# Dense PSUM banks emptied with a priority, one add moved to GpSimd and an early table load in an attention and gated-MLP kernel

## The chip, the cores and the metric

The kernel runs on one core of a Trainium2 chip. The metric is device microseconds of one execution, the median of several. A core has five engines that run their own instruction lists in order: TensorE (PE, matmul), VectorE (DVE), ScalarE (ACT), GpSimd (POOL) and SyncE (SP, which issues the transfers here). They wait for each other by semaphores alone.

## The reference

Banded causal attention with a linear bias, and two gated blocks behind it, all in float32. Batch 4, 8 heads, 576 positions, 64 values a head; the band is 128 wide.

```python
scores = scale * np.matmul(q, k.transpose(0, 1, 3, 2))
scores = np.where(mask, scores + bias[None], -1e9)      # mask: 0 <= i - j < 128
attn = np.exp(scores - np.max(scores, axis=-1, keepdims=True))
x = np.matmul(attn / (np.sum(attn, axis=-1, keepdims=True) + 1e-09), v)   # -> 2304 x 512
x = (1.0 / (1.0 + np.exp(-(x @ w_gate))) * (x @ w_val)) @ w_out   # 512 -> 1536 -> 512
x = ((x @ w1) * (x @ w2)) @ w3 @ w_out2                           # 512 -> 1024 -> 512
```

## The kernel before

The 2304 positions are cut into five blocks (`TILES`: 256, then four of 512), the eight heads into four pairs. Attention is 20 steps, step n being block n // 4 and pair n % 4. A step has three stages that run in different turns of the loop. `stage_s(n)` makes the scores on PE, masks them and adds the bias table on DVE (lines 446 and 449), takes the maximum (455), and on ACT four exponentials for each pair of tiles with their sums (462); then DVE makes the reciprocals (466), and POOL (470) and ACT (472) scale half of the tiles each. `stage_p(n)` transposes the result on PE (480, tiles pt), copies it out on ACT (act_copy, line 69, tiles cp) and zeroes triangles on POOL (484, 488). `stage_pv(n)` multiplies by v on PE (503, tiles pv) and empties that bank into xt as a rounded high part on ACT (69) and a low part on DVE (72). A turn n runs `stage_p(n-2)`, `stage_pv(n-3)`, `stage_s(n)`, and the first seven turns have an order of their own.

The dense work is `layer(grp, blk)`: `gv` makes two products (tiles gv, line 243), empties the first with a sigmoid on ACT (257, tile g), multiplies the second into it on DVE (262), and splits the result into a high part on ACT (69) and a low part on POOL (75, tiles gt); `down1` multiplies by w_out (280, tiles dn) and adds into acc, by an ACT copy for the first group and a DVE add for the others (289). Pieces of `layer` are put between the attention stages by `fill`, as many matmuls as a budget lets in. So PE's order in the attention is written out by hand (`manual_schedule`). On the other engines a scheduler sets the order from a priority, which follows the program's order, and from its own estimate of when an instruction can run.

Transposes, pv, gv and dn all take their PSUM from one ring of four banks, `mm`; the scores have four banks of their own. A matmul group that comes to a bank waits until what lies there has been emptied:

```python
gvpool = ctx.enter_context(
    tc.tile_pool(name="psmm", bufs=4, space=PSUM, side="right", reuse_waits="tile"))
mmpools.append(gvpool)
```

ACT holds one table of functions at a time. The exponential and the sigmoid are in different ones, so every sigmoid in the attention has a load ahead of it (ACT_TABLE_LOAD), and the next exponential another.

The weights arrive as 64-bit floats and are converted by a chain on ACT (115), DVE (116 to 121) and ACT, POOL or DVE again (`convert_next`), with a low priority: `LATER` puts them behind other work. At the start `consts` builds the bias table base on POOL, with one add on DVE (369), and `table(0)` scales it on ACT (404, tiles tab). After the attention all is dense work, and PE's list is the program's order.

Of the kernel before, what the change touches and what calls it, by code (L numbers as in the profile page):

```python
# [9 lines left out]
F32 = mybir.dt.float32  # L10
# [3 lines left out]
AF = mybir.ActivationFunctionType  # L14
ALU = mybir.AluOpType
# [4 lines left out]
P = 128  # L20
# [9 lines left out]

PASSES = ((0, 0), (0, 1), (1, 0))
LATER = 300
FILL = {5: 0.0, 6: 1400.0, 7: 1400.0, 8: 0.0, 9: 0.0, 10: 2700.0, 11: 2700.0}
FULL = 4000.0

# [10 lines left out]
def attn_moe_kernel(  # L46
# [14 lines left out]
    nc = tc.nc  # L61
# [6 lines left out]
    def act_copy(dst, src):  # L68
        nc.scalar.activation(dst, src, AF.Copy)  # L69
# [4 lines left out]
    def pool_lo(dst, src, hi):  # L74
        nc.gpsimd.tensor_tensor(dst, src, hi.bitcast(F32), ALU.subtract)  # L75
# [10 lines left out]
    def cols(blk):  # L86
        return TILES[blk] * P
# [36 lines left out]
    def convert_next():  # L124

        key, _, sink = queue.pop(0)
        with tc.high_priority(offset=-LATER):
            t = staged.pop(key)
# [10 lines left out]
    def convert_start(items):  # L139
        queue.extend(items)  # L140
        for it in queue[:2]:
            if it[0] not in staged:
                fetch(*it[:2])
# [13 lines left out]
    def parts(grp):  # L157
        def src(i, c):
            m = i - NF
            own = (w_gate, w_val, w_out)[c][i] if i < NF else (w1[m], w2[m], w3o[m * P : (m + 1) * P, :])[c]  # L160
            return ahead.get((i, c), own)

        keys = [(i, c) for c in range(3) for i in grp]
        return [(key, src(*key), part_sink) for key in keys]
# [67 lines left out]
    def gv(grp, blk, xs, one):  # L232

        pss = {}
        w = cols(blk)
        ns = w / 2.4 + 13.3

        def product(i, s):
            full = gvpool.tile([P, TB], F32, tag=gvtag, name=f"gv{i}_{blk}_{s}", bufs=gvbufs)
            ps = pss[i, s] = full[:, 0:w]  # L240
            for kk in range(NK):
                for wp, xp in PASSES:
                    nc.tensor.matmul(  # L243
                        ps,
                        wsl[i][:, s, wp, kk * P : (kk + 1) * P],
                        xs[blk][:, xp, kk],
                        start=(kk == 0 and wp == 0 and xp == 0),
                        stop=(kk == NK - 1 and wp == 1),
                    )
                yield 3 * ns  # L250

        g = {}
        for i in grp:
            yield from product(i, 0)
        for i in grp:
            g[i] = m2.tile([P, TB], F32, tag="g", name=f"g{i}_{blk}")[:, 0:w]
            nc.scalar.activation(g[i], pss[i, 0], AF.Sigmoid if one else AF.Copy)  # L257
        ts = []
        for i in grp:
            yield from product(i, 1)  # L260
            pr = g[i]
            nc.vector.tensor_tensor(pr, pr, pss[i, 1], ALU.mult)  # L262
            t = m2.tile([P, 2, TB], F32R, tag="gt", name=f"gt{i}_{blk}", bufs=4)[:, :, 0:w]
            act_copy(t[:, 0], pr)
            pool_lo(t[:, 1], pr, t[:, 0])
            ts.append(t)
        return ts

    def down1(grp, blk, ts):
        first, last = grp[0] == 0, grp[-1] == NF - 1  # L270
        if first:
            acc[blk] = acc_tile(blk, [P, NK, cols(blk)], "acc1")
        if last:
            x2.append(x_tile("x2_", blk))
        for m in range(NK):
            ps = mm_tile([P, TB], f"dn{grp[0]}_{blk}_{m}")[:, 0 : cols(blk)]
            n = 0
            for i, t in zip(grp, ts):
                for wp, xp in PASSES:
                    nc.tensor.matmul(  # L280
                        ps, wsl[i][:, 2, wp, m * P : (m + 1) * P], t[:, xp],
                        start=n == 0, stop=n == 3 * len(grp) - 1,
                    )
                    n += 1
            a = acc[blk][:, m]
            if first:
                act_copy(a, ps)
            else:
                nc.vector.tensor_tensor(a, a, ps, ALU.add)  # L289
            if last:  # L290
                act_copy(x2[blk][:, 0, m], a)
                dve_lo(x2[blk][:, 1, m], a, x2[blk][:, 0, m])
            yield 3 * len(grp) * (cols(blk) / 2.4 + 13.3)
# [36 lines left out]
    def attention(actx, conv):  # L330
        nonlocal spool, gvpool
        cpool = actx.enter_context(tc.tile_pool(name="cpool", bufs=1))
# [15 lines left out]
        def consts():  # L348


            normal0, first, normal, normal2, cross, after, normal3 = (base[:, i] for i in range(7))
            nc.gpsimd.memset(mask, 1)
            nc.gpsimd.affine_select(
                out=mask, in_=mask, compare_op=ALU.is_gt, fill=0.0, base=0, pattern=[[1, P]], channel_multiplier=-1
            )
            for t, k in ((first, 0), (normal, -P)):
                nc.gpsimd.iota(
                    t, pattern=[[1, P]], base=k, channel_multiplier=-1, allow_small_or_imprecise_dtypes=True
                )
            nc.gpsimd.affine_select(  # L360
                out=cross, in_=first, compare_op=ALU.is_ge, fill=0.0, base=0, pattern=[[-1, P]], channel_multiplier=1
            )
            nc.gpsimd.affine_select(
                out=normal, in_=normal, compare_op=ALU.is_gt, fill=0.0, base=0, pattern=[[1, P]], channel_multiplier=-1
            )
            nc.gpsimd.affine_select(
                out=first, in_=first, compare_op=ALU.is_ge, fill=FAR, base=0, pattern=[[-1, P]], channel_multiplier=1
            )
            nc.vector.tensor_tensor(normal, normal, cross, ALU.add)

        def consts2():
            normal0, first, normal, normal2, cross, after, normal3 = (base[:, i] for i in range(7))
# [35 lines left out]
        def load(n):  # L408
            pair, blk, nt, t0, back = where(n)
            t = loads[n]  # L410
            t["k"] = ap2.tile([P, 5 * P], F32, tag="ldk", name=f"ldk{n}")
            t["q"] = ap2.tile([P, 4 * P], F32, tag="ldq", name=f"ldq{n}")

            if not back:
                nc.sync.dma_start(t["k"][:, 0:P], kt[pair, :, t0 * P : (t0 + 1) * P])
            nc.sync.dma_start(t["k"][:, (1 - back) * P : (1 + nt) * P], kt[pair, :, (t0 - back) * P : (t0 + nt) * P])
            nc.sync.dma_start(t["q"][:, 0 : nt * P], qt[pair, :, t0 * P : (t0 + nt) * P])
# [117 lines left out]

        load(0)
        load(1)
        convert_start(parts(groups[0]) + parts(groups[1]) + second_items)
        consts()
        make_identity(nc, ident)  # L540
        table(0)
        with tc.manual_schedule(engines={mybir.EngineType.PE}):
            for n in range(NSTEP + 3):
# [18 lines left out]
                for grp, blk in READY.get(n, ()):  # L562
                    fillers.append(layer(groups[grp], blk))
                fill(FILL.get(n, FULL))
                for _ in range(CONVERT.get(n, 0)):
# [4 lines left out]
    with ExitStack() as conv, ExitStack() as actx:  # L570
        attention(actx, conv)
# [110 lines left out]
```

## Time and profile before

| what | us |
|---|---|
| three runs, median (lowest to highest) | 945.8 (945.59 to 946.12) |
| the profiled execution, its own time | 945.88 |
| its span, first to last instruction | 944.2 |
| PE, ACT, DVE, POOL busy | 897.6, 366.9, 573.5, 290.6 |
| last transposes of the attention start at | 192.5 |
| last pv starts at | 199.7 |
| mean granted TensorE clock | 0.979 |

The span and the execution's own time differ by 1.7 us. The profile shows when each instruction ran and, for idle time ahead of it, whose semaphore ended it. A busy PE is not PE at its peak, since matmuls are pipelined. The granted clock is in shares of full speed, 1.00 for 2.4 GHz; its other level is half of that, and a mean between them is a stretch with both.

### The profile page before, as it was taken

What the parts mean: (1) busy time and instruction counts of PE and PEld (TensorE: products, weight loads), DVE (VectorE), ACT (ScalarE), POOL (GpSimd) and SP (SyncE); (2) the same over time, 40 slices, a digit from 0 to 9 for tenths busy, and PEclk for the clock granted to TensorE, in tenths of its full rate; (3) what the DMA queues carried; (4) which work ended last, traced back from release to release, by engine and by line L of the source; (5) the groups of instructions that cost most, each with busy time, mean ns of one, the idle gap of its engine ahead of it and who ended that gap; (6) DMA issues with size and microseconds to landing.
All of it is one profiled execution on the core that took longest, in us unless ns stands there. A gap on an engine that the chain in (4) does not pass through costs nothing.

```text
span 944.2 us, 12323 instructions
## 1 busy us (share of the span) xinstructions
PE 897.6 (95%) x4528; PEld 736.6 (78%) x4528; DVE 573.5 (61%) x957; ACT 366.9 (39%) x912; POOL 290.6 (31%) x343
## 2 busy tenths in 40 slices
PE   6788786899999999999999999999999999999998
PEld 3456665678878888888888888888888888888887
DVE  5769686525998797698593458943854514422223
ACT  6799897643333332322331244434322312211110
POOL 4567454242422412322322021104422412411111
PEclk9789898999999999999999999999999999999999
DMA  6445353114243243143130122325310300000112
GB/s 185 150 140 161 99 159 119 40 34 145 79 143 113 67 135 101 45 144 113 45 100 23 46 67 101 112 78 156 97 39 1 112 1 1 23 0 1 45 45 112
DMA packets 32604, 79.71 MB, mean 84 GB/s; under 512 B 3616, under 2 KB 5664, under 8 KB 32544
## 3 DMA queue, kind: packets, MB, share of 16 engines
q1 hardware_dynamic: 32544, 78.92, 26.0%
q8 instruction: 36, 0.59, 0.3%
q14 instruction: 24, 0.20, 0.1%
HBM read 65.27 MB, written 13.63 MB: 84 GB/s over the span
## 4 chain that ended last, share of the span: by engine, by line
PE 73%; DVE 11%; ACT 8%; DMA 4%; issue 4%; POOL 1%; SPq 0%; ACTq 0%; POOLq 0%; DVEq 0%
PE gv L243 43%; PE dn L280 11%; PE o L304 10%; PE w3o L209 4%; ACT sm L462 3%; PE pv L503 2%; DVE acc L289 1%; PE s L438 1%; PE pt L480 1%; ACT sm L472 1%; DVE sm L449 1%; DVE s L446 1%; DVE mn L455 1%; ACT cp L69 1%; POOL wsl L75 1%
## 5 line engine op out<-in xcount | busy, mean ns | idle before, releaser
L243 PE MATMUL gv<-xt,wsl 128*128 128x512 f32 (+1 forms) x1440 | 307.6, 372 | 3.2 <-DVE g L262 1.9
L243 PEld LDWEIGHTS gv<-xt,wsl 128*128 128x128 f32 x1440 | 252.5, 191 | 52.7 <-DVE g L262 3.0
L75 POOL TENSOR_TENSOR gt<-g,gt 128x512 fp32r<-128x512 f32 (+1 forms) x100 | 120.5, 1209 | 430.1 <-ACT gt L69 422.8
L243 PE MATMUL gv<-x,wsl 128*128 128x512 f32 (+1 forms) x960 | 200.2, 368 | 0.0
L243 PEld LDWEIGHTS gv<-x,wsl 128*128 128x128 f32 x960 | 167.6, 189 | 30.2
L262 DVE TENSOR_TENSOR g<-g,gv 128x512 f32<-128x512 f32 (+1 forms) x100 | 62.6, 630 | 168.1 <-PE gv L243 151.1
L280 PE MATMUL dn<-gt,wsl 128*128 128x512 f32 (+1 forms) x720 | 156.3, 371 | 5.0 <-ACT cp L69 3.1
L280 PEld LDWEIGHTS dn<-gt,wsl 128*128 128x128 f32 x720 | 126.4, 189 | 30.1 <-ACT cp L69 3.7
L257 ACT ACTIVATE g<-gv 128x512 f32<-128x512 f32 (+1 forms) x100 | 54.7, 550 | 156.1 <-PE gv L243 150.9
L69 ACT ACTIVATE gt<-g 128x512 fp32r<-128x512 f32 (+1 forms) x100 | 58.5, 587 | 145.4 <-DVE g L262 145.2
L304 PE MATMUL o<-wsl,gt 128*128 128x512 f32 x432 | 101.1, 389 | 0.0
L304 PEld LDWEIGHTS o<-wsl,gt 128*128 128x128 f32 x432 | 80.9, 188 | 16.7
L289 DVE TENSOR_TENSOR acc<-acc,dn 128x512 f32<-128x512 f32 (+1 forms) x120 | 74.1, 628 | 21.8 <-PE dn L280 21.5
L313 DVE TENSOR_TENSOR acc<-acc,o 128x512 f32<-128x512 f32 x54 | 37.1, 688 | 35.2 <-PE o L304 35.2
L462 ACT ACTIVATE sm<-sm,mn 128x128 f32<-128x128 f32 x144 | 55.9, 391 | 1.6 <-DVE mn L455 1.0
L503 PE MATMUL pv<-cp,ldv 128*64 128x256 f32 (+1 forms) x352 | 43.4, 382 | 12.6 <-issue 6.9
L503 PEld LDWEIGHTS pv<-cp,ldv 128*64 128x64 f32 x352 | 27.1, 154 | 29.2 <-issue 12.9
L438 PE MATMUL s<-ldk,ldq 64*128 64x256 f32 x288 | 42.1, 434 | 6.3 <-DMA ldq<-in_q_dram 6.3
L470 POOL TENSOR_SCALAR sm<-sm,su 128x128 f32<-128x128 f32 x72 | 32.6, 464 | 41.4 <-DVE su L466 41.4
L209 PE MATMUL w3o<-wo,w3s 128*128 128x512 f32 x192 | 44.4, 390 | 0.2 <-DVE wo L72 0.2
L209 PEld LDWEIGHTS w3o<-wo,w3s 128*128 128x128 f32 x192 | 36.0, 188 | 8.1 <-DVE wo L72 0.7
L438 PEld LDWEIGHTS s<-ldk,ldq 64*128 64x128 f32 x288 | 29.5, 209 | 14.1 <-issue 10.6
(742 smaller groups left out, 868.7 us busy)
## 6 DMA issues: line engine op xcount, KB each, us to landing
ldk<-in_k_dram SPq DMA_DIRECT2D x16, 320.0 KB, 3.0
ldv<-in_v_dram SPq DMA_DIRECT2D x16, 320.0 KB, 2.9
out_dram<-acc SPq DMA_DIRECT2D x18, 256.0 KB, 2.0
ldq<-in_q_dram SPq DMA_DIRECT2D x16, 256.0 KB, 3.3
w3o<-w3os SPq DMA_DIRECT2D x8, 256.0 KB, 2.5
ldk<-in_k_dram SPq DMA_DIRECT2D x4, 128.0 KB, 2.9
ldq<-in_q_dram SPq DMA_DIRECT2D x4, 128.0 KB, 3.0
raw_(0, 0)_99<-in_w_gate_dram SPq DMA_DIRECT2D x1, 512.0 KB, 4.6
```

The costliest lines, as they stand in the source:

```text
L69: nc.scalar.activation(dst, src, AF.Copy)
L75: nc.gpsimd.tensor_tensor(dst, src, hi.bitcast(F32), ALU.subtract)
L209: nc.tensor.matmul(acc2, w3s[u][:, wp, i * P : (i + 1) * P], wo2[kk][:, xp], start=(kk == 0 and wp == 0 and xp == 0), stop=(kk == NC2 - 1 ...
L243: nc.tensor.matmul(ps, wsl[i][:, s, wp, kk * P : (kk + 1) * P], xs[blk][:, xp, kk], start=(kk == 0 and wp == 0 and xp == 0), stop=(kk == N ...
L257: nc.scalar.activation(g[i], pss[i, 0], AF.Sigmoid if one else AF.Copy)
L262: nc.vector.tensor_tensor(pr, pr, pss[i, 1], ALU.mult)
L280: nc.tensor.matmul(ps, wsl[i][:, 2, wp, m * P : (m + 1) * P], t[:, xp], start=n == 0, stop=n == 3 * len(grp) - 1,)
L289: nc.vector.tensor_tensor(a, a, ps, ALU.add)
L304: nc.tensor.matmul(ps, t[:, xp, tt * P : (tt + 1) * P], wsl[i][:, 2, wp], start=n == 0, stop=n == 3 * len(grp) - 1,)
L438: nc.tensor.matmul(ps[:, h, :, u], ld["q"][r, t * P : (t + 1) * P], ld["k"][r, t * P : (t + 2) * P], start=True, stop=True, skip_group_che ...
L462: s["act"] = nc.scalar.activation(y, y, AF.Exp, bias=mn[:, j : j + 1], scale=1.0 / up, accum_out=su[:, j : j + 1])
L503: nc.tensor.matmul(ps[c, a:b], loads[n]["v"][:, j + 1, c], s["cp", h][:, m0 : m0 + b - a], start=j == -back, stop=j == nt - 1, skip_group_ ...
```

## The change

Three edits. The instructions that empty banks of the dense work (sigmoid, multiply, the split, and the add into acc) get a priority 150 places ahead of their place in the program. The add that ends the table base goes from DVE to POOL. An exponential of one column is put on ACT ahead of everything, with a DVE memset for its input.

```diff
+SOONER = 150
@@ gv
-            nc.scalar.activation(g[i], pss[i, 0], AF.Sigmoid if one else AF.Copy)
+            with tc.high_priority(offset=SOONER):
+                nc.scalar.activation(g[i], pss[i, 0], AF.Sigmoid if one else AF.Copy)
@@ gv
-            nc.vector.tensor_tensor(pr, pr, pss[i, 1], ALU.mult)
             t = m2.tile([P, 2, TB], F32R, tag="gt", name=f"gt{i}_{blk}", bufs=4)[:, :, 0:w]
-            act_copy(t[:, 0], pr)
-            pool_lo(t[:, 1], pr, t[:, 0])
+            with tc.high_priority(offset=SOONER):
+                nc.vector.tensor_tensor(pr, pr, pss[i, 1], ALU.mult)
+                act_copy(t[:, 0], pr)
+                pool_lo(t[:, 1], pr, t[:, 0])
@@ down1
-            if first:
-                act_copy(a, ps)
-            else:
-                nc.vector.tensor_tensor(a, a, ps, ALU.add)
+            with tc.high_priority(offset=SOONER):
+                if first:
+                    act_copy(a, ps)
+                else:
+                    nc.vector.tensor_tensor(a, a, ps, ALU.add)
@@ consts
-            nc.vector.tensor_tensor(normal, normal, cross, ALU.add)
+            nc.gpsimd.tensor_tensor(normal, normal, cross, ALU.add)
@@ ahead of convert_start
+        warm = cpool.tile([P, 1], F32, name="warm")
+        nc.vector.memset(warm, 0.0)
+        nc.scalar.activation(warm, warm, AF.Exp)
```

PE's list stays the same but for two matmuls of gv0_4_0. The lists of ACT, DVE, POOL and SP change up to the end of the attention, and hardly after it. Names in the rows below carry the step or the group and block, and a buffer number at the end. ACT keeps its number of table loads, 14. The lines of the changed file stand a few higher: 70 is 69 of before, 259 is 257, 466 is 462, 476 is 472.

First, ACT at steps 4 and 5: sm4 are the exponentials of step 4, cp2 and cp3 the copies of the transposes of steps 2 and 3. Before:

```order
L462 ACTIVATE sm4_314,su4_0_328<-sm4_314,mn4_0_327 128x128 x4
L69 ACTIVATE xt0_278<-pv1_355 128x256
L465 ACTIVATE su4_0_328<-su4_0_328 128x4
L462 ACTIVATE sm4_314,su4_1_343<-sm4_314,mn4_1_342 128x128 x2
L472 ACTIVATE sm4_314<-sm4_314,su4_0_328 128x128 x2
L462 ACTIVATE sm4_314,su4_1_343<-sm4_314,mn4_1_342 128x128 x2
L69 ACTIVATE cp2_0_365<-pt2_0_362 128x2x128
L465 ACTIVATE su4_1_343<-su4_1_343 128x4
L69 ACTIVATE cp2_1_372<-pt2_1_369 128x2x128
L69 ACTIVATE cp3_0_385<-pt3_0_382 128x2x128
```

And of the change:

```order
L70 ACTIVATE wsl0_195<-a_(0, 0)_186 128x512
L70 ACTIVATE xt0_281<-pv1_358 128x256
L70 ACTIVATE cp2_0_368<-pt2_0_365 128x2x128
L70 ACTIVATE cp2_1_375<-pt2_1_372 128x2x128
L70 ACTIVATE cp3_0_388<-pt3_0_385 128x2x128
L466 ACTIVATE sm4_317,su4_0_331<-sm4_317,mn4_0_330 128x128 x4
L70 ACTIVATE cp3_1_395<-pt3_1_392 128x2x128
L469 ACTIVATE su4_0_331<-su4_0_331 128x4
```

The copies cp2 and cp3 went from behind the eight exponentials of step 4 to ahead of them.

Second, ACT where the first sigmoid stands, g0_0, which empties gv0_0_0. Before:

```order
L472 ACTIVATE sm6_495<-sm6_495,su6_1_525 128x128 x2
L257 ACT_TABLE_LOAD
L257 ACTIVATE g0_0_632<-gv0_0_0_538 128x256
L459 ACTIVATE mn7_0_602<-mn7_0_602 128x4
L69 ACTIVATE wsl0_192<-a_(0, 2)_453 128x512
L462 ACT_TABLE_LOAD
L462 ACTIVATE sm7_589,su7_0_603<-sm7_589,mn7_0_602 128x128 x4
```

And of the change:

```order
L463 ACTIVATE mn6_0_511<-mn6_0_511 128x4
L466 ACTIVATE sm6_498,su6_0_512<-sm6_498,mn6_0_511 128x128
L259 ACT_TABLE_LOAD
L259 ACTIVATE g0_0_635<-gv0_0_0_541 128x256
L476 ACTIVATE sm5_406<-sm5_406,su5_1_436 128x128 x2
L466 ACT_TABLE_LOAD
L466 ACTIVATE sm6_498,su6_0_512<-sm6_498,mn6_0_511 128x128 x3
L463 ACTIVATE mn6_1_527<-mn6_1_527 128x4
```

It went from between two softmaxes into that of step 6, and with it both table loads; half of sm5's scaling (line 476) now stands behind the sigmoid.

Third, ACT at step 13: acc1_1 are the four copies that empty dn0_1_0 to dn0_1_3. Before:

```order
L69 ACTIVATE acc1_1_1282<-dn0_1_0_1283 128x512
L459 ACTIVATE mn13_0_1248<-mn13_0_1248 128x4
L69 ACTIVATE acc1_1_1282<-dn0_1_1_1288 128x512
L462 ACT_TABLE_LOAD
L462 ACTIVATE sm13_1235,su13_0_1249<-sm13_1235,mn13_0_1248 128x128 x4
L459 ACTIVATE mn13_1_1264<-mn13_1_1264 128x4
L69 ACTIVATE acc1_1_1282<-dn0_1_2_1293 128x512
L465 ACTIVATE su13_0_1249<-su13_0_1249 128x4
```

And of the change:

```order
L70 ACTIVATE xt2_985<-pv10_1225 128x512
L70 ACTIVATE wsl1_737<-a_(1, 2)_937 128x512
L70 ACTIVATE acc1_1_1285<-dn0_1_0_1286 128x512
L70 ACTIVATE acc1_1_1285<-dn0_1_1_1291 128x512
L463 ACTIVATE mn13_0_1251<-mn13_0_1251 128x4
L70 ACTIVATE acc1_1_1285<-dn0_1_2_1296 128x512
L466 ACTIVATE sm13_1238,su13_0_1252<-sm13_1238,mn13_0_1251 128x128
L70 ACTIVATE acc1_1_1285<-dn0_1_3_1301 128x512
L466 ACTIVATE sm13_1238,su13_0_1252<-sm13_1238,mn13_0_1251 128x128 x3
```

Two of the copies came out from behind the exponentials of step 13, and the table load went away from ahead of them (it stands in step 12 now).

## Rows read from the trace of the kernel before

**Rows 1.** The page: the span.

```profile
span 944.2 us, 12323 instructions
```

**Rows 2.** Windows: us, then busy time of PE, PEld, DVE, ACT, POOL, PEclk, DMA.

```profile
24.00:48.00 24.00, 17.64 (x114) 11.84 (x112) 17.79 (x35) 17.39 (x76) 13.72 (x26) 0.79 0.43 142
48.00:96.00 48.00, 40.35 (x284) 29.03 (x280) 39.41 (x73) 44.71 (x164) 33.63 (x59) 0.89 0.49 160
206.00:300.00 94.00, 92.08 (x439) 76.89 (x438) 77.64 (x125) 30.09 (x53) 29.57 (x23) 1.00 0.37 121
300.00:944.20 644.20, 640.23 (x3048) 539.19 (x3047) 362.54 (x581) 177.44 (x305) 155.03 (x124) 1.00 0.21 67
```

**Rows 3.** PE's waits up to 206 us: us in total, times, longest.

```profile
PE pv L503 <- issue: 6.9, 3, 3.1
PE pv L503 <- POOL cp L488: 5.4, 4, 2.6
```

**Rows 4.** DVE at the start, timeline: start, us, instruction, idle before.

```profile
7.00 0.29 DVE L369 TENSOR_TENSOR base<-base 128x128 f32<-128x128 f32 x1
8.46 0.70 DVE L446 COPY_PREDICATED s<-mask,s 128x512 f32<-128x512 int32 x1 [1.17 <-PE s L438]
9.42 0.69 DVE L449 SCALAR_TENSOR_TENSOR sm<-s,tab 128x512 f32<-128x512 f32 x1 [0.26 <-ACT tab L404]
```

**Rows 5.** The page: groups by line, busy and mean ns of one.

```profile
L75 POOL TENSOR_TENSOR gt<-g,gt 128x512 fp32r<-128x512 f32 (+1 forms) x100 | 120.5, 1209 | 430.1 <-ACT gt L69 422.8
L462 ACT ACTIVATE sm<-sm,mn 128x128 f32<-128x128 f32 x144 | 55.9, 391 | 1.6 <-DVE mn L455 1.0
```

**Rows 6.** PE in order of time.

```profile
23.73 0.86 PE L503 MATMUL pv<-cp,ldv 128*64 128x256 f32 x6 [0.33 <-POOL cp L488]
...
31.86 1.54 PE L503 MATMUL pv<-cp,ldv 128*64 128x256 f32 x6 [1.09 <-POOL cp L488]
33.33 3.79 PE L438 MATMUL s<-ldk,ldq 64*128 64x256 f32 x16
...
38.35 1.09 PE L480 MATMUL pt<-ident,sm 128*128 128x128 f32 x8
39.37 2.00 PE L438 MATMUL s<-ldk,ldq 64*128 64x256 f32 x16
...
45.65 1.95 PE L503 MATMUL pv<-cp,ldv 128*64 128x128 f32 x20
...
97.36 2.93 PE L243 MATMUL gv<-xt,wsl 128*128 128x256 f32 x12 [1.01 <-ACT acc L69]
...
115.06 1.95 PE L503 MATMUL pv<-cp,ldv 128*64 128x128 f32 x20 [2.93 <-issue]
...
125.04 1.95 PE L503 MATMUL pv<-cp,ldv 128*64 128x128 f32 x20 [0.92 <-issue]
...
159.73 1.94 PE L480 MATMUL pt<-ident,sm 128*128 128x128 f32 x8 [6.93 <-ACT acc L69]
...
175.11 3.38 PE L503 MATMUL pv<-cp,ldv 128*64 128x128 f32 x20 [3.07 <-issue]
...
199.68 1.95 PE L503 MATMUL pv<-cp,ldv 128*64 128x128 f32 x20
```

**Rows 7.** ACT in order of time.

```profile
27.89 0.37 ACT L69 ACTIVATE cp<-pt 128x256 f32<-128x256 f32 x1
...
50.61 1.28 ACT L257 ACT_TABLE_LOAD   x1
51.90 0.38 ACT L257 ACTIVATE g<-gv 128x256 f32<-128x256 f32 x1
...
114.39 0.57 ACT L69 ACTIVATE acc<-dn 128x512 f32<-128x512 f32 x1
...
159.01 2.04 ACT L69 ACTIVATE acc<-dn 128x512 f32<-128x512 f32 x4
...
174.41 0.60 ACT L257 ACTIVATE g<-gv 128x512 f32<-128x512 f32 x1
```

## The prediction

> **What bounds the kernel now.** The execution took 945.88 us, 1.7 more than its span [rows 1], and the median of the three runs is 945.8; I reckon from 945.9. First I read busy time by stretch. From 300 us on PE is busy 640.2 of 644.2 us, from 206 to 300 us 92.1 of 94 [rows 2]: dense work, nothing to win. So the change can only be worth what it pulls forward the last pv of the attention, which starts at 199.7 [rows 6]. What stands behind it (weights by DMA, ACT and POOL, then DVE's conversions) is released by ACT and POOL work that itself waits for these last banks, so I let all of it move along with PE.
>
> Next I read PE's waits up to 206 us [rows 3]. They are short and spread: for a bank that ACT has not emptied, for triangles on POOL, for the scaling of the softmax. The reader is to see that there is no single one. Last comes the order of time on PE and ACT [rows 6, 7]: each long wait is an ACT list that does exponentials first, and a copy that PE needs behind them. ACT itself is busy 44.7 of the 48 us from 48 to 96 [rows 2]; there its work in sum, not its order, is close to the limit.
>
> **The method.** I walk the new lists in order, each instruction with its duration in the trace, and write down when PE reaches certain groups. Shifts are against the trace of before; minus is earlier. Copies are 0.37 for 256 columns, 0.57 for 512; four exponentials 4 x 0.39 = 1.56 [rows 5, 7].
>
> **The start (+1.6).** The add on DVE took 0.29 [rows 4]. On POOL no such row exists; a POOL add of 512 columns takes about 1.2 [rows 5]. Between 0.29 and 1.2 I take a quarter of 1.2, 0.3, by columns; either end is free, since DVE's second mask copy comes at 8.46 anyway [rows 4]. The added memset and exponential of one column have no rows either; nothing and the 0.39 of a full exponential [rows 5] bound them, and either is free while the first transfers run. The scale-and-add of step 0 waits today for the table, to 9.42. But DVE's new list has the second mask copy ahead of it, as the old one, and that ends at 8.46 + 0.70 = 9.16 [rows 4]. So the early table load, 1.28, is worth only 0.26. It is more than lost: the first reciprocal now stands behind step 2's mask copy and scale-and-add on DVE, and the second copy of step 0's transposes behind step 2's exponentials on ACT. My walk has pv1's last six matmuls at 25.3, not 23.73 [rows 6].
>
> **Steps 2 to 4 (-4.8).** Today cp2 stands behind eight exponentials of step 4 and comes at 27.89 [rows 7]; pv2's last six run at 31.86, and PE is then at its lower clock (0.79 in the mean from 24 to 48 us [rows 2]): the 16 score matmuls at 33.33 take 3.79, those at 39.37 2.00 [rows 6]. In the new list cp2 comes right behind pv1's copy. That copy ends at 26.6, cp2's first at 27.0, and POOL's four triangles of 0.4 follow without a scaling between: pv2's last at 28.6. Scores then end at 31.4, and step 4's exponentials (27.8 on), its reciprocals and scaling at 33.5, when pt4 can end what starts today at 38.35.
>
> **Steps 5 to 8 (half of it is given back).** g0_0 and two loads, 1.28 + 0.38 + 1.28 = 2.9, move into step 6's softmax, ahead of the ACT half of step 5's scaling and of most of step 6's exponentials. So pt5's last tiles wait for ACT, until 43.3 in my walk, and pv4 starts at 43.6 where it starts at 45.65 now [rows 6]: -2.0. Its cover before was that both loads stood where only step 7 waited; step 7 gets them back, and its transposes come 2.5 earlier.
>
> **Steps 9 to 12 (-5.3).** ACT runs through here nearly without idle time in both lists. g0_1's loads move up by one softmax in the same manner. Then the exponentials of step 11 and the copies cp10, for whose banks dn0_0 waits, come some 5 us earlier, and the four acc1_0 copies stand together. gv1_0_0, now at 97.36 [rows 6], starts at 92.1.
>
> **Steps 13 and 14 (-8.3, then -6.6).** pv11 waits 2.93 for a bank that the third acc1_1 copy frees, at 114.39, behind a load and four exponentials [rows 6, 7]. In the new list this copy is ahead of both: 1.28 + 1.56 = 2.8 less, pv11 at 106.8 for 115.06. But pv12 waits for g0_2, which keeps its place behind step 14's exponentials, so ACT, not PE, sets it: 118.4 for 125.04. 1.7 are given back as idle time.
>
> **Steps 15 to 18 (-7.4).** The adds into acc1_0 come without a scale-and-add and a maximum between them (-0.5). The largest wait, 6.93 at 159.73, stays: the acc1_2 copies (159.01) stand behind step 17's softmax in both lists [rows 6, 7]. It lasts from step 17's scores on, so it moves with them; DVE no longer holds step 17's first scale-and-add for a reciprocal, some 0.6.
>
> **Steps 19 to 22 (-10.3).** pv16 waits 3.07 for g0_3, which ends behind four exponentials at 174.41 + 0.60 [rows 6, 7]. The new list has it ahead of them and of one scaling: 1.56 + 0.34 = 1.9, to -9.4. Step 19 needs no load ahead of its exponentials any more; its last transposes come another 0.9 earlier, and the last pv with them: 189.4 for 199.7 [rows 6].
>
> The walk takes 0.1 for a hand-over between engines. At 9.16 to 9.42 one takes 0.26 [rows 4]; some twelve hand-overs stand on this way, 12 x 0.15 = 1.8 less gain. **Sum: 945.9 - 10.3 + 1.8 = 937.4, and I say 937.5.** A measurement of this kernel can tell about 0.2%, 1.9 us, from no change.
>
> **The price of a switch.** Each pair of loads is priced at 2 x 1.28: the sigmoid starts 0.01 after its load ends [rows 7], so nothing else is paid. The Trainium skill (ScalarE: Activation LUTs, What ACT_TABLE_LOAD costs) gives 1.28 us for a load and 1.38 for a drain with it; by that, the three pairs that now stand ahead of a wait of PE (g0_0, g0_1, g1_0) would cost 3 x 2 x 1.38 = 8.3 more, and the sum would be about 945.8. The trace does not agree: no 1.38 lies beside this load.
>
> **Rivals.**
> *ACT takes it back* (0.16). From 48 to 96 us ACT has only 3.3 us of idle time [rows 2]. If the lead of steps 2 to 4 is used up there, what stays is the bank waits behind it: 2.8 at pv11 less 1.7 at pv12, 1.9 at pv16, 0.6: 942.3. For it speaks the half given back already at step 5; against it that DVE and PE, not ACT, hold several of those exponentials today.
> *Nothing happens* (0.09). The sum of ACT's work and loads is the same and the longest wait stays. If each wait of PE only moves to the next bank or the next scaling, 945.9 within 1.5. Against it: the copies at 27.89 and 114.39 stand behind work that the next PE group doesn't need.
> *A switch costs more in the middle of a softmax* (0.02). If ACT stood still for as long again as the load, 1.28, whenever it changes table between exponentials, the three pairs would cost 3 x 2 x 1.28 = 7.7 more: 945.2. The 0.01 above speaks against it [rows 7]. It is the drain of the skill's section named above.
> *Slower: loads in the middle of a softmax* (0.09). Each early sigmoid puts 2.9 us into a softmax whose scaling the next transposes wait for. It is free as long as PE's groups up to those transposes take longer than that. It decides at step 5: if pt4 is not early, by pv2 still late behind POOL, the 1.6 of the start stay, pt5 ends 2.8 later than now, and the wait that grows at pv12 is 1.7 beyond today's, with 2.8 back at pv11: 945.9 + 1.6 + 2.8 + 1.7 - 2.8 = 949.2.
> *My forecast, faster by 4.5 to 13* (0.64). More than the walk is possible if PE keeps its clock where it loses it today: the 20 matmuls at 175.11 take 3.38 and those at 115.06 1.95 [rows 6], 1.4 each time, at two or three places.
>
> **How the numbers follow.** The likeliest case gives 937.5, its own range 932 to 941.5. Below 932 only several more stretches at full clock lead: 0.06. Up to 944.5 lie nearly all of the first rival and a part of the others. So the range is 932 to 944.5, which leaves out some 2 in 10. Faster by over 0.2% (under 944): my forecast, nearly all of the first rival and a little of the second, 0.80. Within 0.2%: most of the second and the third, 0.11. Slower: 0.09.
>
> **What would show it.** In the trace of the change: pt4 near 34 and the scores of step 5 at 2.0; pv4 near 43.6 (the loss at step 5); gv1_0_0 near 92; no wait ahead of pv11, but one of over 2 ahead of pv12; still some 7 us ahead of pt16; about 1 ahead of pv16; the last pv near 190. From there to the end the distance should be the same as now, 944.2 - 199.7 = 744.5; if it grew, DVE's conversions would have become late, and the forecast would be wrong in that step. It would be wrong in the first step if the scores of step 5 ran at the lower clock or pv2 came after 30.

## The result, and the profile after

The changed kernel takes 936.36 us (median of 4 runs, 935.53 to 939.69); the kernel before, timed beside it, 945.96 (4 runs, 945.59 to 946.89). The ratio is 0.9904, 95% interval 0.9879 to 0.9929: faster, as forecast, and 1.1 us from the 937.5 that was said. The profiled execution took 935.53, its span 933.8.

The stretches, as in [rows 2]: length, then busy time of PE, PEld, DVE, ACT, POOL, granted clock, DMA share, GB/s.

```profile
24.00:48.00 24.00, 19.19 (x130) 13.26 (x128) 20.34 (x39) 20.78 (x78) 15.82 (x30) 0.88 0.54 172
48.00:96.00 48.00, 39.68 (x290) 28.97 (x289) 37.14 (x72) 44.24 (x167) 33.33 (x61) 0.95 0.46 143
196.00:290.00 94.00, 94.00 (x454) 79.42 (x453) 78.70 (x127) 32.18 (x56) 30.02 (x23) 1.00 0.38 123
290.00:933.80 643.80, 639.70 (x3042) 538.23 (x3040) 361.06 (x579) 176.86 (x305) 154.93 (x124) 1.00 0.21 67
```

The dense part is as it was (639.70 for 640.23 us of PE). ACT still has under 4 us to spare from 48 to 96. The third line is new: PE is busy in all 94 us behind the attention, where it lacked 1.9 before [rows 2].

PE's waits up to 196 us (us in total, times, longest):

```profile
PE pt L484 <- POOL sm L474: 10.7, 8, 2.5
...
PE pt L484 <- ACT acc L70: 5.9, 1, 5.9
PE pv L507 <- POOL cp L492: 3.2, 2, 2.5
PE dn L283 <- ACT cp L70: 2.8, 1, 2.8
PE gv L244 <- ACT acc L70: 2.3, 1, 2.3
PE pv L507 <- ACT g L259: 1.5, 1, 1.5
PE pv L507 <- issue: 1.3, 1, 1.3
```

"issue" stands for idle time in which the profile shows nothing that PE waited for. Of the 6.9 us of it ahead of a pv [rows 3] 1.3 are left under that name and 1.5 for g. The dn wait for cp was there before too (3.1 us in two waits, at dn0_0; now 2.8 in one, at dn0_2). The gv wait for acc has grown from 1.0 to 2.3, and the pt wait for the scaling on POOL, now the largest, from 6.2 to 10.7.

PE in order of time, with the groups that [rows 6] has of before:

```profile
26.64 1.20 PE L507 MATMUL pv<-cp,ldv 128*64 128x256 f32 x8
31.09 2.00 PE L442 MATMUL s<-ldk,ldq 64*128 64x256 f32 x16
33.82 0.44 PE L484 MATMUL pt<-ident,sm 128*128 128x128 f32 x2
...
42.86 1.18 PE L484 MATMUL pt<-ident,sm 128*128 128x128 f32 x4 [2.50 <-POOL sm L474]
45.00 2.79 PE L507 MATMUL pv<-cp,ldv 128*64 128x128 f32 x20
...
94.69 4.55 PE L244 MATMUL gv<-xt,wsl 128*128 128x256 f32 x24 [2.33 <-ACT acc L70]
108.79 1.95 PE L507 MATMUL pv<-cp,ldv 128*64 128x128 f32 x20
119.34 1.95 PE L507 MATMUL pv<-cp,ldv 128*64 128x128 f32 x20 [1.49 <-ACT g L259]
...
139.20 1.95 PE L507 MATMUL pv<-cp,ldv 128*64 128x128 f32 x20
146.78 1.67 PE L283 MATMUL dn<-gt,wsl 128*128 128x512 f32 x6 [2.81 <-ACT cp L70]
155.47 1.94 PE L484 MATMUL pt<-ident,sm 128*128 128x128 f32 x8 [5.88 <-ACT acc L70]
168.65 1.95 PE L507 MATMUL pv<-cp,ldv 128*64 128x128 f32 x20 [1.26 <-issue]
191.97 1.95 PE L507 MATMUL pv<-cp,ldv 128*64 128x128 f32 x20
```

ACT in order of time (some table loads, sigmoids and copies), beside [rows 7]:

```profile
42.28 1.28 ACT L259 ACT_TABLE_LOAD   x1
43.57 0.38 ACT L259 ACTIVATE g<-gv 128x256 f32<-128x256 f32 x1
...
139.87 1.28 ACT L466 ACT_TABLE_LOAD   x1 [1.71 <-DVE mn L459]
154.75 2.04 ACT L70 ACTIVATE acc<-dn 128x512 f32<-128x512 f32 x4
...
167.95 0.60 ACT L259 ACTIVATE g<-gv 128x512 f32<-128x512 f32 x1
```

The walk's places against the trace (us; the shift against before in brackets):

| place | before | forecast | after |
|---|---|---|---|
| step 5's scores, duration | 3.79 | 2.00 | 2.00 |
| pt4 | 38.35 | 33.5 (-4.8) | 33.82 (-4.5) |
| pv4 | 45.65 | 43.6 (-2.0) | 45.00 (-0.65) |
| gv1_0_0 | 97.36 | 92.1 (-5.3) | 94.69 (-2.7) |
| pv11 | 115.06, waits 2.93 | 106.8 (-8.3), no wait | 108.79 (-6.3), no wait |
| pv12 | 125.04, waits 0.92 | 118.4 (-6.6), waits over 2 | 119.34 (-5.7), waits 1.49 |
| pt16 | 159.73, waits 6.93 | -7.4, waits some 7 | 155.47 (-4.3), waits 5.88 |
| pv16 | 175.11, waits 3.07 | -9.4, waits some 1 | 168.65 (-6.5), waits 1.26 |
| last pv | 199.68 | 189.4 (-10.3) | 191.97 (-7.7) |
| from there to the end | 744.5 | 744.5 | 741.8 (-2.7) |

The last two rows add up to the 10.4 by which the span shrank, 944.2 to 933.8. Shape and waits are those of the walk; its leads are 1 to 3 us too long from step 5 on, and 2.7 came behind the attention, where nothing was forecast. Between the places shown the lead was gone twice: pv5 starts at 52.76 for 52.34 before, and pv9 at 86.55 for 85.65. All of what is left at the end was won from step 11 on.

### The profile page after: what moved, and what is told of

The parts are those of the page before. It is cut to its first block, busy times and chain, and to the rows that moved or that the text cites. A ratio compares the mean times of both kernels' runs of the same rounds, so it can differ in the third digit from the quotient of the medians.

```text
span 933.8 us, 12319 instructions
## 1 busy us (share of the span) xinstructions
PE 891.2 (95%) x4528; PEld 733.2 (79%) x4528; DVE 571.9 (61%) x957; ACT 367.9 (39%) x913; POOL 290.4 (31%) x344
## 4 chain that ended last, share of the span: by engine, by line
PE 80%; ACT 6%; DVE 6%; DMA 3%; POOL 2%; issue 1%; SPq 0%; DVEq 0%; ACTq 0%
PE gv L244 48%; PE dn L283 14%; PE o L308 10%; PE w3o L210 4%; ACT sm L466 2%; PE pv L507 2%; PE s L442 2%; PE pt L484 1%; ACT sm L476 1%; DVE sm L453 1%; DVE s L450 1%; DMA early<-a_('ahead', 2, 1)_1306 1%; DMA ldq<-in_q_dram 1%; POOL sm L474 1%; POOL cp L492 1%
## 5 line engine op out<-in xcount | busy, mean ns | idle before, releaser
L244 PE MATMUL gv<-x,wsl 128*128 128x512 f32 (+1 forms) x960 | 200.2, 368 | 0.0
L507 PE MATMUL pv<-cp,ldv 128*64 128x256 f32 (+1 forms) x352 | 39.7, 365 | 6.0 <-POOL cp L492 3.2
L474 POOL TENSOR_SCALAR sm<-sm,su 128x128 f32<-128x128 f32 x72 | 31.3, 447 | 33.5 <-DVE su L470 33.5
L484 PE MATMUL pt<-ident,sm 128*128 128x128 f32 x144 | 24.9, 301 | 17.1 <-POOL sm L474 10.7
```

Source lines behind the costliest of these rows:

```text
L244: nc.tensor.matmul(ps, wsl[i][:, s, wp, kk * P : (kk + 1) * P], xs[blk][:, xp, kk], start=(kk == 0 and wp == 0 and xp == 0), stop=(kk == N ...
L507: nc.tensor.matmul(ps[c, a:b], loads[n]["v"][:, j + 1, c], s["cp", h][:, m0 : m0 + b - a], start=j == -back, stop=j == nt - 1, skip_group_ ...
```

## The experiments

All were timed beside the kernel before, in three series on three chips, in which it had medians of 945.88, 945.43 and 945.10. "pv" times are from the one profiled execution of each.

**Series 1: the parts.** Each kernel is the changed one without some of its edits:

```diff
 e1_start_only: no high_priority at all (base add on GpSimd and early exponential stay)
 e2_sooner_only:
-            nc.gpsimd.tensor_tensor(normal, normal, cross, ALU.add)
+            nc.vector.tensor_tensor(normal, normal, cross, ALU.add)
-        warm = ...; memset; activation(warm, warm, AF.Exp)
 e3_gv_only (in down1):
-            with tc.high_priority(offset=SOONER):
                 act_copy(a, ps)  /  nc.vector.tensor_tensor(a, a, ps, ALU.add)
 e4_acc_only (in gv): both "with tc.high_priority(offset=SOONER):" taken away
```

Only the start. 

> The add of the table base on GpSimd and the early exponential alone; nothing has the new priority. On ScalarE the rows up to step 5 are then those of the changed kernel, the rest those of the kernel before. First theory (the lead of steps 2 to 4 doesn't last): pt4 is early as after the change (near 34 where it was 38.35), but by pv5 and pv6 PE is within 1 us of before, and the time is 945 to 947, within 0.2% of before. Second theory (the prediction's walk: lead is lost only because g0_0 and two loads move into step 6's softmax): without that move the 4.5 us stay up to the last pv, and the time is 940 to 942.

Only the priority. 

> The priority on all bank emptying alone; the add of the base stays on VectorE and there is no early exponential, so ScalarE's rows up to step 5 are those of before. First theory: the whole gain comes from the order from step 6 on, and the time is 935.5 to 938, as after the change. Second theory (leads add up): without the 4.5 us of steps 2 to 4, g0_0's two loads make pt5 late by 2.8 and the time is 940 to 942. A third, from the rival that ended slower: with no lead at step 5 the early loads cost more than they bring, 946 to 949.

Start, and the gate and value part. 

> The changed kernel, but the copies and adds into acc1 without the priority (only the sigmoid, the product with the value and the two halves of gt have it). First theory (the sum is made of single waits): pv11 waits nearly 3 us again for the third acc1_1 copy, and of the 9.5 us gained 2.5 to 3 are lost: 939 to 940. Second theory (ScalarE's total work sets the stretch, a wait removed comes back behind it): pv12 takes over what pv11 loses, and the time stays within 1 us of the changed kernel, 936 to 937.5.

Start, and acc1. 

> The start edits and the priority on the copies and adds into acc1 alone; sigmoid, product and gt without it. First theory (single waits): no wait ahead of pv11, but pv16 waits about 3 us for g0_3 and pv16 runs at the lower clock, so 2.8 of the gain come: 942 to 943.5. Second theory (what counts is g, since the next layer's products wait for it): as before within 0.2%, 944.5 to 947.

| kernel | median us (runs) | ratio to before, interval | last pv |
|---|---|---|---|
| start only | 943.36 (12) | 0.9979, 0.9966 to 0.9992 | 200.9 |
| priority only | 938.68 (6) | 0.9932, 0.9918 to 0.9945 | 194.7 |
| start, gate and value | 938.70 (12) | 0.9938, 0.9918 to 0.9957 | 193.4 |
| start, acc1 | 943.15 (12) | 0.9978, 0.9966 to 0.9991 | 200.8 |

The start is worth about 2 us by its ratio, the priority 6.4 (0.0068 of 945.9); together 8.4 of the whole change's 9.1 by its ratio. That is between the theories for both kernels: the lead of steps 2 to 4 is neither lost altogether nor kept. In the profile of the start alone it goes where it goes in the changed kernel, though no table load has moved (this execution, 945.58, is one of its longer ones, and its last pv is 1.2 late; where the others have their 2 us is not shown):

```profile
34.19 0.44 PE L481 MATMUL pt<-ident,sm 128*128 128x128 f32 x2
...
43.22 1.67 PE L481 MATMUL pt<-ident,sm 128*128 128x128 f32 x6 [2.49 <-POOL sm L471]
44.82 3.68 PE L504 MATMUL pv<-cp,ldv 128*64 128x128 f32 x20
...
53.39 1.95 PE L504 MATMUL pv<-cp,ldv 128*64 128x128 f32 x20
```

pt4 is 4.2 early, pv4 0.8, and pv5 (52.3 before) 1.1 late; the 20 pv matmuls behind the wait take 3.68 for 1.95 (the granted clock from 24 to 48 us is 0.86 in the mean). So the lead can go without the loads of g0_0. But they are not free either: with the priority only, pt5's last two tiles wait 0.95 for ACT's scaling, which stands behind the load and the sigmoid, and pv4 is 1.9 late.

acc1 alone gives nothing beside the start (943.15 for 943.36), although its local effect is as forecast: pv11 waits 0.46, not 2.92. By pv12 it is gone (125.9, against 126.1 with the start alone): in the gv ahead of it PE waits 1.87 for ACT's copy of xt. So the time lies in the first theory's range, but by the start's 2 us. Beside the gate and value part acc1's priority may be worth up to 2 (938.70 to 936.36), but these are medians of different series and the intervals of the ratios overlap, so it is not shown. In the profile without it pv11 comes 1.4 later than with the change (110.16 for 108.79) and pv12 0.7.

**Series 2: which of the gate's pieces, and what the switches cost.**

```diff
 e7_gt_plain (in gv):
-            with tc.high_priority(offset=SOONER):
                 nc.vector.tensor_tensor(pr, pr, pss[i, 1], ALU.mult)
                 act_copy(t[:, 0], pr)
                 pool_lo(t[:, 1], pr, t[:, 0])
 e8_g_plain (in gv):
-            with tc.high_priority(offset=SOONER):
                 nc.scalar.activation(g[i], pss[i, 0], AF.Sigmoid if one else AF.Copy)
 e9_no_switch (in gv, beside the attention):
-                nc.scalar.activation(g[i], pss[i, 0], AF.Sigmoid if one else AF.Copy)
+                nc.scalar.activation(g[i], pss[i, 0], AF.Exp)
 e10_exp_form (in gv, beside the attention):
+                nc.scalar.activation(g[i], pss[i, 0], AF.Exp, scale=-1.0)
+                nc.vector.tensor_scalar(g[i], g[i], 1.0, None, ALU.add)
+                nc.vector.reciprocal(g[i], g[i])
```

Without the priority on product and gt. 

> The changed kernel with the priority on the sigmoids and on the copies and adds into acc1, but not on the product with the value and the two halves of gt. First theory (the early sigmoid with its two table loads is what PE gains from; it frees the bank and lets the product follow): 936 to 938, pv12's and pv16's waits as after the change. Second theory (what the next down-product waits for is gt, and gt is what the priority moves): most of the 7 us that the gate and value part brought go, 941 to 943.5, and dn0_0 waits again near 93.

Without it on the sigmoids. 

> The changed kernel with the priority on the product, on gt and on acc1, but not on the sigmoids, so that the table loads stand where they stood before. First theory (the early sigmoid): pv16 waits about 3 us for g0_3 as before, dn0_0 about 2, and the time is 941 to 943.5. Second theory (gt): 936 to 938.

No table switches. 

> The changed kernel with an exponential in place of the sigmoid in all gate layers that run beside the attention, so no table is switched until the attention is over and 12 loads of 1.28 us are gone from ScalarE; the gate value there is not the sigmoid, which leaves out that part of the reference. First theory (the prediction's price: three pairs stand ahead of a wait of PE, 3 x 2 x 1.28 = 7.7): at least 4 of it come back, 928 to 932.5. Second theory (where the pairs stand, VectorE's and GpSimd's part of the softmax ends last anyway): within 1.5 us of the changed kernel, 935 to 938.

No switches, sigmoid kept by VectorE. 

> The same without a switch, but with the sigmoid kept: ScalarE takes exp(-x), VectorE adds one and takes the reciprocal (two more instructions of up to 512 columns for each gate bank beside the attention; the like of them, a tensor_scalar of 512 columns, takes 0.42 us in the trace of before, a copy under a mask 0.70). First theory: ScalarE's relief outweighs VectorE's 0.9 to 1.4 per bank, 930 to 934. Second theory: VectorE, busy about 37 of 48 us between 48 and 96, becomes what the softmax waits for, 938 to 943.

| kernel | median us (runs) | ratio to before, interval | last pv |
|---|---|---|---|
| product and gt plain | 936.10 (5) | 0.9906, 0.9890 to 0.9923 | 192.7 |
| sigmoids plain | 945.49 (12) | 1.0000, 0.9989 to 1.0011 | 201.8 |
| no switch (Exp) | 928.36 (4) | 0.9820, 0.9802 to 0.9838 | 183.3 |
| exp form, reciprocal | 934.54 (4) | 0.9883, 0.9866 to 0.9899 | 190.9 |

The first two settle it: without the priority on product and gt nothing is lost, without that on the sigmoids everything is, the start's 2 us too, which is more than either theory had. Where it comes about is seen on ACT around g0_1 (the two executions profiled took 947.38 with the sigmoids plain, one of the longer ones, and 935.74 with them early). With the sigmoids plain (a load for the sigmoid, a load for the next exponentials, and step 11's first exponential):

```profile
81.94 1.28 ACT L258 ACT_TABLE_LOAD   x1
...
87.05 1.28 ACT L465 ACT_TABLE_LOAD   x1
88.34 0.40 ACT L465 ACTIVATE sm<-sm,mn 128x128 f32<-128x128 f32 x1
```

and PE behind it, waiting for the copies cp10 that stand behind these exponentials:

```profile
91.14 0.62 PE L282 MATMUL dn<-gt,wsl 128*128 128x256 f32 x3 [1.52 <-ACT cp L70]
95.50 1.85 PE L282 MATMUL dn<-gt,wsl 128*128 128x256 f32 x6 [3.73 <-ACT cp L70]
```

With the sigmoids early (product and gt plain), in the same order:

```profile
77.95 1.28 ACT L259 ACT_TABLE_LOAD   x1
...
80.53 1.28 ACT L465 ACT_TABLE_LOAD   x1
...
85.70 0.39 ACT L465 ACTIVATE sm<-sm,mn 128x128 f32<-128x128 f32 x1
```

The pair now stands within step 10's softmax and is 4.0 and 6.5 earlier; step 11's exponentials start 2.6 earlier, and dn0_0's matmuls run without a wait. The early pair has a price one step ahead, where pt10 waits for step 10's scaling (with the sigmoids plain it does not wait):

```profile
86.35 1.11 PE L483 MATMUL pt<-ident,sm 128*128 128x128 f32 x6 [1.93 <-POOL sm L473]
```

So pv9 starts 2.2 later than with the sigmoids plain. From pv9 to pv10 PE then needs 12.1 us (87.4 to 99.5) for 18.4 (85.2 to 103.6): 6.3 in one step, 4.0 net of that price. By the last pv the two differ by 9.1; the rest comes at pv12 (2.5) and from pv15 to pv17 (4.2), less 1.6 lost at other places. The pair is not all that moved: between the plain sigmoid and its second load ACT also ran two weight copies and a conversion (0.62, 0.62 and 0.70), which the early order has elsewhere. How much of the 6.3 is theirs was not taken apart.

The loads still cost. Without them the kernel is another 8 us faster, of the 12 x 1.28 = 15.4 that go from ACT; its time lies in the first theory's range. The exp form keeps the gate and gets 2 of them: VectorE pays for it. Its groups up to 200 us (busy, mean ns of one, idle before):

```profile
L263 DVE RECIPROCAL g<-g 128x512 f32<-128x512 f32 x5 | 16.7, 3346 | 0.1
...
L263 DVE RECIPROCAL g<-g 128x256 f32<-128x256 f32 x2 | 3.5, 1739 | 0.0
L262 DVE TENSOR_SCALAR g<-g 128x512 f32<-128x512 f32 x5 | 2.1, 422 | 2.2 <-ACT g L261 2.2
```

The expectation had 0.9 to 1.4 us per bank for the two instructions; it is 3.3 + 0.4.

**Series 3: order against loads, and a faster kernel.** The Trainium skill (ScalarE: Activation LUTs, Table sets: the hidden batching unit) lists tanh in the set that holds exp, so a gate written as (1 + tanh(x/2))/2 should need no switch. The trace agrees: the kernel below with tanh holds two loads up to 200 us, at 0.80 and at 188.59, where the changed one holds 14.

```diff
 e11_tanh (changed kernel; only beside the attention):
-                nc.scalar.activation(g[i], pss[i, 0], AF.Sigmoid if one else AF.Copy)
+                nc.scalar.activation(g[i], pss[i, 0], AF.Tanh, scale=0.5)
-                nc.vector.tensor_tensor(pr, pr, pss[i, 1], ALU.mult)
+                nc.vector.scalar_tensor_tensor(pr, pr, 1.0, pss[i, 1], ALU.add, ALU.mult)
-                    act_copy(a, ps)
+                    nc.scalar.activation(a, ps, AF.Copy, scale=0.5)
-                    nc.vector.tensor_tensor(a, a, ps, ALU.add)
+                    nc.vector.scalar_tensor_tensor(a, ps, 0.5, a, ALU.mult, ALU.add)
 e12_convert_later (changed kernel):
-        CONVERT = {1: 1, 3: 1, 5: 1, 8: 1, ...
+        CONVERT = {1: 1, 5: 2, 8: 1, ...
 e13_sigmoid_alone (kernel before):
+            with tc.high_priority(offset=150):
                 nc.scalar.activation(g[i], pss[i, 0], AF.Sigmoid if one else AF.Copy)
 e14_before_no_switch (kernel before, beside the attention):
-            nc.scalar.activation(g[i], pss[i, 0], AF.Sigmoid if one else AF.Copy)
+            nc.scalar.activation(g[i], pss[i, 0], AF.Exp)
```

Tanh. 

> The changed kernel with the gate beside the attention as (1 + tanh(x/2)) / 2: a tanh on ScalarE for the sigmoid, the one added in the same VectorE instruction as the product, the half taken where acc1 is copied or added, so no instruction is added. The program then holds two table loads instead of 14. First theory (the loads are what the kernel without a switch won): 927 to 930. Second theory (a tanh or the three-operand product takes longer, or another wait steps in): 931 to 936.

Conversion of w_val later. 

> The changed kernel with the conversion of group 0's w_val moved from behind step 3 to behind step 5 (two conversions there, none at step 3), so that step 5's softmax has no conversion between its rows on VectorE and GpSimd. First theory (the lead of steps 2 to 4 is eaten by the conversion that the new order pushes into step 5's softmax, and would be eaten by it anywhere before step 8): pt5's last tiles 1 to 2 us earlier than 42.86, but pv6 where it was and 935 to 937.5. Second theory (it costs because of its place): the last pv 1.5 to 2.5 earlier, 933 to 935.

The sigmoids' priority alone. 

> The kernel before with the priority on the sigmoids alone: no other line is changed, so base, table load, product, gt and acc1 are those of before. First theory (the sigmoid's place is the change's gain, the start and acc1 add about 2 us): 937.5 to 940. Second theory (it needs the early copies into acc1 beside it): 941 to 944.

No switch, old order. 

> The kernel before with an exponential in place of the sigmoid in the layers beside the attention, so without their 12 table loads (the gate value there is not the sigmoid, which leaves out that part of the reference); no priority anywhere. First theory (the priority is worth what it is because of where the pair of loads stands): without loads the order matters little, 928 to 931. Second theory (a sigmoid behind the exponentials holds PE's bank whatever it costs itself): the loads' 8 us come off, but the 7 to 9 of the priority stay lost, 935 to 939.

| kernel | median us (runs) | ratio to before, interval | last pv |
|---|---|---|---|
| tanh | 928.22 (4) | 0.9809, 0.9788 to 0.9831 | 183.6 |
| conversion later | 943.72 (11) | 0.9973, 0.9956 to 0.9991 | 200.2 |
| sigmoids' priority alone | 938.16 (6) | 0.9919, 0.9899 to 0.9939 | 193.5 |
| before, no switch | 938.74 (6) | 0.9920, 0.9901 to 0.9938 | 192.4 |

One added line in the kernel before, the priority on the sigmoid, gives 7 of the change's 9.6 us: the first theory for that kernel. Taking the loads away in the old order gives 6.4, and the loads away together with the whole change 17: the second theory for the last kernel, by its time. So the change and the loads add nearly in full. Where the change wins is another matter. From pv9 to pv10 the two kernels without loads need 15.7 us (old order) and 15.0: at the place where the early sigmoid won most, the order is worth 0.7 once the loads are gone, as the first theory had it. What the change still brings without loads comes elsewhere, among others at pv11 (2.43 us of waiting for an acc1 copy in the old order, none in the new) and between pv14 and pv15 (13.1 us for 8.6). Which of its edits does that was not tested.

Tanh beats both kernels: 17 us under before, 8 under the change. Its gain over the change is not spread over its loads: a lead of 2.6 at pv12 is lost again by pv13, ahead of which a dn waits 2.49 for DVE's product. Step 17, in PE's order (pv14, dn0_2, pt16, pv15):

```profile
139.86 1.95 PE L518 MATMUL pv<-cp,ldv 128*64 128x128 f32 x20
...
143.67 2.33 PE L292 MATMUL dn<-gt,wsl 128*128 128x512 f32 x9
...
147.54 1.04 PE L495 MATMUL pt<-ident,sm 128*128 128x128 f32 x8
148.51 1.95 PE L518 MATMUL pv<-cp,ldv 128*64 128x128 f32 x20
```

and ACT there (step 16's first exponential, three of the acc1_2 copies, the fourth, and step 17's first exponential):

```profile
137.32 0.40 ACT L477 ACTIVATE sm<-sm,mn 128x128 f32<-128x128 f32 x1 [0.36 <-DVE mn L470]
...
144.67 1.97 ACT L300 ACTIVATE acc<-dn 128x512 f32<-128x512 f32 x3 [0.72 <-PE dn L292]
...
149.34 0.58 ACT L300 ACTIVATE acc<-dn 128x512 f32<-128x512 f32 x1
149.82 0.39 ACT L477 ACTIVATE sm<-sm,mn 128x128 f32<-128x128 f32 x1
```

Up to pv14 this kernel is 0.7 later than the change (139.86 for 139.20), though nine of the change's switches no longer stand on ACT up to there. At pv15 it is 8.8 earlier (148.51 for 157.34): dn0_2 no longer waits 2.81, pt16 no longer 5.88. Step 16's exponentials start at 137.32, where the change had a load at 139.87 ahead of them, and in ACT's list the acc1_2 copies now stand ahead of step 17's softmax, where the change had them behind it (154.75). How much is the load itself and how much the new place of the copies was not taken apart.

The conversion that was moved is the miss of this series; both theories had it harmless. pt5 waits less for POOL, but its last two tiles then wait for ACT's scaling, and behind that PE stands still for the weights:

```profile
41.60 1.21 PE L484 MATMUL pt<-ident,sm 128*128 128x128 f32 x4 [1.73 <-POOL sm L474]
43.87 0.77 PE L484 MATMUL pt<-ident,sm 128*128 128x128 f32 x2 [1.06 <-ACT sm L476]
...
54.83 0.51 PE L244 MATMUL gv<-xt,wsl 128*128 128x256 f32 x2 [4.33 <-ACT wsl L70]
56.64 2.50 PE L244 MATMUL gv<-xt,wsl 128*128 128x256 f32 x10 [1.31 <-POOL wsl L76]
```

So the conversion within step 5's softmax accounts for 0.8 of the 2.5 that pt5 waits for POOL. The 1.06 behind it are what the prediction spoke of: ACT's half of the scaling stands behind g0_0's load (at 41.84) and the sigmoid. In the changed kernel, with the conversion in its place, that wait is 0.27. Either of the two is enough to hold PE here, and with the conversion gone pv4 is only 0.4 earlier than with the change. pv5 comes 8.0 later (60.8 for 52.8), the last pv 8.2, and the kernel takes 7.4 more. The one other place that was tried is worse, and a delay at pv5 reaches the end nearly whole.

## Why the prediction was right, step by step

**The start (+1.6).** Mis-sized: all eight matmuls of pv1 run from 26.64, so the last six are at least 2.9 late, not 1.6. pv2 comes at 29.94 for 28.6, just ahead of the 30 that was to show this step wrong. It didn't reach pt4, which is where it was forecast.

**Steps 2 to 4 (-4.8).** Right in mechanism and size: pt4 4.5 early, the scores of step 5 in 2.00. What it is worth at the end was mis-sized: about 2, by the start alone (0.9979, interval 0.9966 to 0.9992) and by the change against the priority alone (936.36 and 938.68, in different series).

**Steps 5 to 8 (half given back).** The step whose cause was incomplete. It said that the loads of g0_0 take the lead, by making pt5 wait for ACT. In the changed kernel that wait is 0.27, and the long one is for POOL, 2.50. The start alone, and the kernel with no switch (pt5 at 44.0 after a wait of 2.49), have that without the loads. Before, a wait stands there too:

```profile
44.60 1.11 PE L480 MATMUL pt<-ident,sm 128*128 128x128 f32 x6 [1.39 <-POOL sm L470]
```

Of the 1.1 that it grew, 0.8 is the weight conversion; the rest stays open. What the prediction meant is real where the conversion is out of the way (1.06) or the lead is missing (0.95 with the priority only). The size was wrong too: pv4 is 0.65 early, not 2.0, partly because pt5 runs slower (its last six tiles take 1.18 + 0.77 for 1.11), and pv5 is 0.4 late.

**Steps 9 to 12 (-5.3).** The place and the size of this step were right, and it is the heart of the change: pv10 comes 3.7 earlier than before, with the early pair of g0_1. From pv9 to gv1_0_0 3.6 are gained, where the walk's shifts differ by 3.3. But pv9 is 0.9 late, where the walk came to this step with the lead of 2.0 that it had at pv4: pt10 waits 1.94 behind that pair, a price the walk had not put in. So gv1_0_0 is 2.7 early and not 5.3.

**Steps 13 and 14.** Both waits as forecast in kind, none at pv11 and 1.49 at pv12 (over 2 was said). But the 2.8 at pv11 that the walk gives to the acc1_1 copies are not theirs to keep: with the start and these copies alone the gain of pv11 is gone at pv12.

**Steps 15 to 18 (-7.4).** -4.3. (The terms that the prediction names, 6.6, 0.5 and 0.6, give 7.7 and not 7.4; so do 5.3 and 2.8 give 8.1 for the 8.3 ahead of it.) The wait at pt16 stayed, 5.88; a new one of 2.81 at dn0_2 was not in the walk. The copy cp15 for which it waits stands behind step 16's softmax, and ahead of that stands g1_1's second load, which began only when DVE's maximum was there. In the kernels without loads this wait is gone; as the copies into acc1_2 moved there too, the load's own part is not shown.

**Steps 19 to 22 (-10.3).** Right in the wait: pv16 waits 1.26. Its matmuls take 1.95 for 3.38 [rows 6], which the prediction had not in its sum but as something that could bring more. The last pv -7.7.

**The distance to the end (unchanged).** Wrong by 2.7. Of these, 1.9 are what PE lacks in the third line of [rows 2], where the prediction saw nothing to win. They are waits for DVE, gone after the change; before:

```profile
PE gv L243 <- DVE g L262: 1.9, 2, 1.1
```

Over all these profiles the distance lies between 741.3 and 745.6, and 2.0 us of such waits stand in one without any priority and none in another; so it is not shown that the change made it. Why DVE is late there in some of them stays open.

**Hand-overs (+1.8).** They were to stand for what the walk missed, which at the last pv is 2.6, 0.8 more. With that and the 2.7 behind, 937.4 + 0.8 - 2.7 = 935.5, the time of the profiled execution: two errors of opposite sign, and the total is closer than its parts. So the closeness, 1.1 us, is in part luck.

**The price of a switch.** No drain is to be seen beside the loads: 42.28 + 1.28 = 43.56, and the sigmoid starts at 43.57. The drain that the Trainium skill (ScalarE: Activation LUTs, What ACT_TABLE_LOAD costs) adds to a switch does not show here, and the 945.8 that it would have given did not come. That answers the rival of the dearer switch as well: the second load of that pair ends at 44.55 + 1.28 = 45.83, and the exponential starts at 45.85.

The rival "ACT takes it back" has the right engine: that ACT's time counts is what the kernels without loads show. But it does not win, since the order counts as well. The rival with loads in mid softmax has a real price in it (0.95 at pt5 with the priority only, 1.9 at pt10) but too little on the other side. It needed pt4 not to be early. Priority alone had that (pv4 at 47.5, 1.9 late; pv9 3.5 late) and was 6.4 us faster by its ratio still: its price was paid at steps 5 and 10 and outweighed at step 11 (pv10 1.0 early). "Nothing happens" is out by the interval of the result.

## What to carry to other kernels

When a priority moves many instructions, try them one by one: here one line carried most of it, and a wait that another one removed came back one group later. Ask first whether a switched table can be avoided by a function that shares the table in use; beside the reordering that was worth another 8 us, nearly as much again, and most of it came at one place. A lead counts only if the next shared stage isn't late for another reason, while here a delay in the same place went through to the end. And look one step ahead of the gain for its price: where the early order saved 6.3 us, it cost 2.2 at the transposes just before.

## What the runs showed of the hardware

- A table load is not always hidden beneath the wait of the instruction that needs it. In the changed kernel the one at 139.87 came after 1.71 us of idle time that DVE's maximum ended, and then took its 1.28 ahead of the exponential. In the kernel before, the one at 139.42 ran ahead of the wait: its sigmoid started at 141.95, after 1.25 us of idle time that PE's gv ended. What decides between the two is not shown. All loads of these two profiles take 1283 ns.
- A reciprocal of 128x512 on VectorE takes 3346 ns in the kernel with the exp form, 1739 at 256 columns, where adding a constant takes 422 at 512: 6.3 ns for each further column (1607 / 256).
- Tanh runs off the table that exp has loaded: the kernel with it holds two loads up to 200 us, one at its start and one after its last exponentials, where before and after hold 14.
